# Scaling w1 and w2 apart, through a shared float32 staging, with the first x2 block taken in early

## The chip, the cores and the metric

One core of one Trainium2 chip runs the whole program. The time is that of one execution on the device, in microseconds (us), and the median over several runs is compared. The engines are PE (matrix products), DVE (vector), ACT (activations, scaled copies), POOL (a second elementwise engine) and SP, whose queue issues the DMAs. Every engine takes its instructions in the order in which the program lists them.

## What is computed

Three stages in a row, in float32 to the outside:

```python
q_pool = q.reshape(B, H, S // 2, 2, D).mean(axis=3)       # 4 batches, 8 heads, 1152 keys, D = 64
attn   = softmax(q_pool @ k.T / sqrt(D))
x      = (attn @ v)  as (2304 tokens, 512)
h = x @ w_in;  x = (h * sigmoid(h)) @ w_out               # "MoE1": 512 -> 2048 -> 512
h = (x @ w1) * (x @ w2) @ w3                              # "MoE2": 512 -> 1024, 1024 -> 1024
out = h @ w2_out                                          # 1024 -> 512
```

The weights arrive as float64. The kernel multiplies w3 by w2_out first (eight products of line 1172), so MoE2 has two steps for a block of tokens: the products with w1 and w2, and one with the joint matrix w3 w2_out.

## The kernel before

**Numbers.** Most products are made from pairs of float16 parts, a high and a low one, in three terms (high by high, high by low, low by high). To split an array it is scaled by a power of two that comes from its largest magnitude. That costs a fixed chain, written once as `top_mm` (line 380) with `pow2` (line 372): a maximum along each partition, a small product on PE that spreads the 128 maxima to all partitions (line 385, two matmul instructions), a second maximum on DVE (line 388), and four or five tiny DVE instructions that make the scale. Then ACT writes the high part, and DVE the low one as the scaled difference.

**float64 weights.** A tile of 128 by 512 float64 words is loaded into a buffer `v64` (line 1071), POOL shapes the low words (line 403), ACT the high words (line 409), and DVE merges both in two instructions (lines 413 and 414). For w1 and w2 the result lands in float32 staging tiles `w32`, sixteen of them in the kernel before; ACT then takes their maxima (line 1082). Only when all sixteen are there does `split16` (line 1037) make one scale, `ws2`, for both matrices and split them into `w1h` and `w2h` (lines 1051 and 1058). w2_out becomes `wor` (lines 1092 and 1097), w3 becomes `w3t` (lines 1152 and 1157).

**Blocks.** MoE1 works on nine blocks of 256 tokens (products of lines 816 and 857) and stores its output to memory in HBM, `x2d` (line 872). MoE2 works on six blocks of 384 tokens: `x2s` is loaded (line 1256), its maximum is taken (line 1276) and spread (line 385), the parts `x2h` are written (lines 1290 and 1270), then eight pairs of products follow (line 1311, twelve matmuls each), whose results are evacuated by ACT into `asb` (line 1330) and multiplied by DVE into `abf` (line 1335); the split of that into `abr` feeds the products of line 1389, whose results ACT evacuates (line 1406) and SP stores.

**Room.** SBUF is reused in steps. When the last attention buffer is done, `opened` (line 1012) lets the pools of MoE2's weights be laid over the attention's, and six more PSUM banks (`mt`) become free for products. When MoE1's input weights have been used for the last time, `x2_room` (line 1137) opens the room for `x2s`, `x2h` and `x2m`. When all of MoE1 is done, `done1` opens the room for w3 and the products' results. `blocks` (line 1227) later hands the sixteen `w32` tiles to `abr` and `abf` as eight further buffers each.

**Order.** The order of the instructions is not written by hand. Each step is an operation of a class `Plan` with an engine, an assumed cost, a key and its dependences. `go` (line 176) places operations one by one, always the one that can start first, by key among equals; the order of their planned starts is the order in the program, on all engines at once. `run` repeats this with keys disturbed by the seeded draws listed in `DRAWS` (line 31). So an assumed cost has no effect on the chip but through the order: an operation whose inputs are later on the chip than in the plan makes its engine wait, with all that is queued behind it. The plan's cost for a merge of a float64 tile is 1.65 us (line 418), for the maximum of an x2 block 1.75 us (line 1275).

## Time and profile before

| | us |
|---|---|
| median of 3 runs | 1133.23 (1132.26 to 1133.62) |
| the profiled execution, its own time | 1134.38 |
| its span, first to last instruction | 1132.6 |
| PE busy | 1081.3 |
| DVE busy | 786.5 |
| ACT busy | 695.6 |
| POOL busy | 158.4 |

The profile has one row for each instruction or group of instructions. A row of the timeline gives the start, the duration, the engine, the line, the operation and what it writes from what; in square brackets stands how long the engine sat idle before it, and what ended that. The view of the chain that ended last follows the work back from the last instruction, so that its pieces add up to the span. A view by stretches gives busy times of the engines and the TensorE clock that was granted, as a share of full speed.

### The profile page before, as it was taken

To read this page: it belongs to the slowest core of one execution; us is meant where nothing else is said; L and a number is where in the kernel's file an instruction comes from. 1 tells how busy PE (TensorE), PEld (TensorE's weight loads), DVE (VectorE), ACT (ScalarE), POOL (GpSimd) and SP (SyncE) were. 2 spreads that over 40 slices of the span, in tenths; PEclk is the share of its full clock that TensorE was granted. 3 is DMA by queue.
4 is the path that set the end of the run, shared out by engine and by line. 5 is a ranking of instruction groups with operands and counts; after the bars stand their busy time and mean duration, and the time that the engine had idled before them with its cause. 6 is when DMAs were issued, how large, how long until landed. Compare 5 with 4: busy or idle time off the path is not lost. (4 is left out here: it accounts for less than half of the span.)

```text
span 1132.6 us, 22742 instructions
## 1 busy us (share of the span) xinstructions
PE 1081.3 (95%) x9354; PEld 822.7 (73%) x9354; DVE 786.5 (69%) x1291; ACT 695.6 (61%) x1103; POOL 158.4 (14%) x150
## 2 busy tenths in 40 slices
PE   6767999999999999999999999997999999999998
PEld 5556877788888888887887888886777655556553
DVE  6998996698688898788997784779855542332211
ACT  5767686687687687686877775675644542433322
POOL 1311210021110011120030120555110000000000
PEclk9988999999999999999999999998999999999999
DMA  9746334598989999889999788566331010100001
GB/s 369 268 141 235 129 120 161 124 180 172 199 156 190 224 184 224 183 163 198 216 192 179 138 140 155 202 207 190 128 112 29 29 56 1 56 19 10 28 1 56
DMA packets 294823, 163.21 MB, mean 144 GB/s; under 512 B 256064, under 2 KB 266816, under 8 KB 294720
## 3 DMA queue, kind: packets, MB, share of 16 engines
q1 hardware_dynamic: 294720, 161.77, 59.9%
q8 instruction: 73, 1.20, 0.4%
q14 instruction: 30, 0.25, 0.1%
HBM read 80.22 MB, written 9.44 MB: 79 GB/s over the span
## 5 line engine op out<-in xcount | busy, mean ns | idle before, releaser
L628 DVE TENSOR_REDUCE sm<-sc 128x1 f32<-128x1152 f32 x144 | 192.8, 1351 | 49.2 <-PE sc L582 48.9
L603 ACT ACTIVATE e<-sc,sm 128x1152 f32<-128x1152 f32 x144 | 175.3, 1218 | 77.3 <-DVE sm L628 67.6
L582 PE MATMUL sc<-kt,qt 64*128 64x384 f32 (+3 forms) x1280 | 185.6, 429 | 10.1 <-DMA kt<-in_k_dram 6.4
L857 PEld LDWEIGHTS <-w 128*128 128x128 f16 x1728 | 166.5, 99 | 30.4 <-issue 10.4
L816 PEld LDWEIGHTS <-w 128*128 128x128 f16 x1728 | 167.2, 98 | 28.2 <-issue 8.5
L857 PE MATMUL mm<-g,w 128*128 128x256 f16 x1536 | 181.9, 275 | 0.4 <-ACT x32t L759 0.4
L841 POOL TENSOR_TENSOR g<-t,g 128x512 f16<-128x512 f32 x72 | 97.7, 1363 | 537.0 <-ACT g L838 528.0
L582 PEld LDWEIGHTS sc<-kt,qt 64*128 64x128 f32 (+1 forms) x1280 | 139.2, 178 | 44.3 <-issue 17.6
L614 DVE SCALAR_TENSOR_TENSOR p<-e,sm,p 128x1152 f16<-128x1152 f32 x108 | 153.9, 1440 | 16.8 <-ACT p L649 16.3
L816 PE MATMUL mm<-x,w 128*128 128x256 f16 x1416 | 164.3, 275 | 0.3 <-DVE x L748 0.2
L649 ACT ACTIVATE p<-e,sm 128x1152 f16<-128x1152 f32 x108 | 133.0, 1248 | 17.6 <-DMA pt<-p 13.1
L733 PE MATMUL mm<-pt,v 128*64 128x256 f16 (+1 forms) x1944 | 89.1, 248 | 4.5 <-DMA pt<-p 3.2
L733 PEld LDWEIGHTS <-v 128*64 128x64 f16 x1944 | 80.7, 111 | 13.1 <-issue 9.2
L1311 PEld LDWEIGHTS <-w1h 128*128 128x128 f16 x576 | 56.1, 98 | 37.9 <-issue 0.8
L1311 PEld LDWEIGHTS <-w2h 128*128 128x128 f16 x576 | 56.0, 98 | 37.5 <-issue 1.1
L1311 PE MATMUL mt<-x2h,w2h 128*128 128x384 f16 x456 | 78.4, 326 | 0.0
L1311 PE MATMUL mt<-x2h,w1h 128*128 128x384 f16 x420 | 73.0, 326 | 0.0
L640 PE MATMUL sc<-identr,e 128*128 128x128 f32 x324 | 47.3, 299 | 20.0 <-ACT e L603 17.4
L640 PEld LDWEIGHTS sc<-identr,e 128*128 128x128 f32 x324 | 39.7, 153 | 26.9 <-ACT e L603 21.4
L832 ACT ACTIVATE t<-mm,xm 128x512 f32<-128x512 f32 x59 | 40.4, 685 | 25.3 <-PE mm L816 20.4
L838 ACT ACTIVATE g<-t 128x512 f16<-128x512 f32 x72 | 44.0, 623 | 8.5 <-DVE t L835 8.5
L643 ACT COPY pt<-sc 128x1152 f32<-128x1152 f32 x36 | 39.8, 1114 | 14.3 <-PE sc L640 13.9
(182 smaller groups left out, 1306.1 us busy)
## 6 DMA issues: line engine op xcount, KB each, us to landing
v<-in_moe_w_dram SPq DMA_DIRECT2D x32, 512.0 KB, 4.2
qs<-in_q_dram SPq DMA_DIRECT2D x16, 640.0 KB, 4.9
kt<-in_k_dram SPq DMA_DIRECT2D x16, 576.0 KB, 4.9
qs<-in_q_dram SPq DMA_DIRECT2D x16, 512.0 KB, 4.5
g<-in_moe_w_in_dram SPq DMA_DIRECT2D x16, 512.0 KB, 5.8
w<-t SPq DMA_DIRECT2D x32, 256.0 KB, 3.1
stage<-in_v_dram SPq DMA_DIRECT2D x12, 576.0 KB, 5.0
x2d<-t SPq DMA_DIRECT2D x36, 128.0 KB, 2.3
```

Of the source, the lines that this page charges most:

```text
L582: return nc.tensor.matmul(sc.t[cols, bank, x0 - bank * (S // 3) : x1 - bank * (S // 3)], qt.t[rows * D : (rows + 1) * D, 4 if last else 2 ...
L603: nc.scalar.activation(e.t.rearrange("p (a x) -> p a x", a=3), flat(), AF.Exp, bias=sm.t[:, 0:1], accum_out=sm.t[:, 1:2])
L614: nc.vector.scalar_tensor_tensor(p16.t[:, 1], e.t, sm.t[:, 3:4], p16.t[:, 0], op0=ALU.mult, op1=ALU.subtract)
L628: DVE, 1.36, lambda: nc.vector.tensor_reduce(sm.t[:, 0:1], flat(), axis=AX.XY, op=ALU.max, negate=True),
L640: nc.tensor.transpose(to[:, c * P : (c + 1) * P], e.t[:, c * P : (c + 1) * P], ident)
L649: ACT, 1.27, lambda: nc.scalar.activation(p16.t[:, 0], e.t, AF.Copy, scale=sm.t[:, 3:4]),
L733: nc.tensor.matmul(ps.t[a * D : (a + 1) * D, :nn], v16.t[:, a, c, tv, :], rhs, start=idx == 0, stop=idx == 3 * NK - 1,)
L816: nc.tensor.matmul(ps.t[:, f % 2 * BL : (f % 2 + 1) * BL], w16[0][ct * NQ + f // 4][:, tw, (f % 4) * P : (f % 4 + 1) * P], x16.t[:, ct, tx ...
L838: nc.scalar.activation(gv(0), two(g32), AF.Copy)
L841: nc.gpsimd.tensor_tensor(gv(1), two(g32), gv(0), op=ALU.subtract)
L857: nc.tensor.matmul(ps.t[:, :BL], w16[1][f][:, tw, ct * P : (ct + 1) * P], gs[u].t[:, f % 4, tg, :], start=f == 0 and n == 0, stop=f == NF ...
L1311: nc.tensor.matmul(ps.t[:, :TB], buf.t[:, ct, tw, f * P : (f + 1) * P], xr.t[:, ct, tx, :], start=idx == 0, stop=idx == 11,)
```

## The change

- **Two scales.** The jobs for w1 come first, then those for w2, with half of the w2_out tiles behind each. `split16` runs twice, over eight staging tiles each, with a scale `ws2s[0]` for w1 and `ws2s[1]` for w2. A block's output scale becomes two columns (one more small DVE instruction for each block); the evacuation of w1's products uses one, that of w2's the other.
- **Shared staging.** `w32` has eight tiles in place of sixteen. w2's tiles go where w1's were, so a merge for w2 waits until a tile of w1 has been split.
- **First x2 block early.** `x2s`, one `x2h` buffer and `x2m` move into a pool that is laid when `opened` allows it. The load and the maximum of an x2 block depend on `opened` where they depended on `x2_room`; the second `x2h` buffer still comes with `x2_room`.
- **Further buffers.** `abr` takes its eight further buffers from the eight `w32` tiles, `abf` takes its eight from the `v64` tiles, after the last float64 tile has been read.
- **The schedule.** In the plan, the spreading product of `top_mm` is taken as ready 3.0 us after the maximum that it reads (`SLACK`). The plan's cost of a merge becomes 1.95 us for the jobs of w1, w2, w2_out and w3, and 1.60 us for MoE1's (1.65 us for all before). `DRAWS` is another list, of 33 seeds in place of 23, so the order of the whole program is another.

```diff
@@ -28,9 +28,11 @@
 ENGINES = (PE, ACT, DVE, POOL, SP)
 LOAD_AFTER = 3.0
+SLACK = 3.0
 DRAWS = (
...
 SWITCH = 0.1
 AFTER = {PE: 0.25, ACT: 0.2, DVE: 0.15, POOL: 0.2, SP: 0.0}
@@ -65,7 +67,7 @@
 class Op:
     __slots__ = (
         "eng", "cost", "land", "fn", "key", "after", "need", "ready", "start", "end", "takes", "bufs", "n", "hook",
-        "placed", "mode", "frees",
+        "placed", "mode", "frees", "slack",
     )
@@ -79,7 +81,7 @@
         o = Op()
         o.eng, o.cost, o.land, o.fn, o.key = eng, cost, land, fn, key
         o.after, o.need, o.ready, o.takes, o.bufs, o.placed = [], 0, 0.0, [], [], []
-        o.n, o.hook, o.mode = len(self.ops), None, mode
+        o.n, o.hook, o.mode, o.slack = len(self.ops), None, mode, 0.0
         before = set()
         seen = set()
         for items, write in ((r, False), (w, True)):
@@ -237,7 +239,7 @@
                     buf.tag.free[buf.place] = buf.end
                     buf.tag.last[buf.place] = buf.users
             for x in o.after:
-                x.ready = max(x.ready, o.end + (0.0 if x.eng == e and o.land is None else AFTER.get(e, 0.0)))
+                x.ready = max(x.ready, o.end + x.slack + (0.0 if x.eng == e and o.land is None else AFTER.get(e, 0.0)))
                 x.need -= 1
                 if x.need == 0:
                     cand[x.eng].append(x)
@@ -386,9 +388,10 @@
             [r], [am], key,
         )
         op(DVE, 0.22, lambda: nc.vector.reduce_max(dst(), am.t[:, :P], axis=AX.X), [am], [w], key)
+        spread.slack = SLACK
         return spread
-    def from_f64(dst, words, dst_b, words_b, key):
+    def from_f64(dst, words, dst_b, words_b, key, cost=1.6):
@@ -415,7 +418,7 @@
         op(POOL, 0.8, top3, [], [(words_b, 0)], key - 0.5)
         op(ACT, 0.68, rebias, [(words_b, 1)], [dst_b], key)
-        op(DVE, 1.65, merge, [(words_b, 0), (words_b, 1)], [dst_b], key + 0.01)
+        op(DVE, cost, merge, [(words_b, 0), (words_b, 1)], [dst_b], key + 0.01)
     tiles = []
@@ -988,9 +991,9 @@
     pools = {}
     t_w1, t_w2, t_wor = Tag(1), Tag(1), Tag(1)
-    t_w32 = Tag(4 * NC)
-    ws2 = const.tile([P, 5], F32, name="ws2")
-    ws2_b, wm2_b, wm2 = Buf(Tag(1)), Buf(Tag(1)), wmx[0]
+    t_w32 = Tag(2 * NC)
+    ws2s = [const.tile([P, 5], F32, name=f"ws2_{n}") for n in range(2)]
+    ws2_bs, wm2_b, wm2 = [Buf(Tag(1)) for _ in range(2)], Buf(Tag(1)), wmx[0]
     assert NF == 4 * NC
     t_w64b, t_wfb = Tag(4), Tag(4, fifo=False)
     NR = 3
@@ -1003,12 +1006,17 @@
         pw = pools["pw"] = tc.alloc_tile_pool(name="pw", bufs=1, side="left")
         t_w1.tiles = [pw.tile([P, NC, 2, NF2 * P], F16, name="w1h")]
         t_w2.tiles = [pw.tile([P, NC, 2, NF2 * P], F16, name="w2h")]
-        t_w32.tiles = [pw.tile([P, 512], F32, name=f"w32_{i}") for i in range(4 * NC)]
+        t_w32.tiles = [pw.tile([P, 512], F32, name=f"w32_{i}") for i in range(2 * NC)]
         pf = pools["pf"] = tc.alloc_tile_pool(name="pf", bufs=1, side="left")
         t_wor.tiles = [pf.tile([P, NF2, 2, DM], F32R, name="wor")]
         t_w64b.tiles = [pf.tile([P, 512, 2], I32, name=f"v64_{i}") for i in range(4)]
         t_wfb.tiles = [pf.tile([P, 512], F32, name=f"wfb_{i}") for i in range(4)]
-
+        t_x2s.tiles = [pf.tile([P, NC, TB], F32, name="x2s")]
+        t_x2h.tiles = [pf.tile([P, NC, 2, TB], F16, name="x2h_0")]
+        t_x2m.tiles = [pf.tile([P, 6], F32, name=f"x2m_{i}") for i in range(2)]
+
+    TB = 3 * P
+    t_x2s, t_x2h, t_x2m = Tag(1), Tag(1), Tag(2)
     opened = control(attn_bufs, to_moe2, hook=lambda at: t_mm.free.update({2 + i: at for i in range(6)}))
     attn_end = B * TPB + 2.0
@@ -1019,24 +1027,29 @@
     w1_b, w2_b, wo_b = Buf(t_w1), Buf(t_w2), Buf(t_wor)
     jobs = []
-    for ct in range(NC):
-        for wsrc, buf in ((w1, w1_b), (w2, w2_b)):
+    for n, (wsrc, buf) in enumerate(((w1, w1_b), (w2, w2_b))):
+        for ct in range(NC):
             for u in range(2):
                 cs = slice(512 * u, 512 * (u + 1))
                 jobs.append((wsrc[ct * P : (ct + 1) * P, cs], buf, ct, cs))
-    for j in range(NF2):
-        jobs.append((w2_out[j * P : (j + 1) * P, :], wo_b, j, slice(0, DM)))
+        for j in range(NF2 // 2 * n, NF2 // 2 * (n + 1)):
+            jobs.append((w2_out[j * P : (j + 1) * P, :], wo_b, j, slice(0, DM)))
     for f in range(NF2):
         for u in range(2):
             jobs.append((w3[f, u], None, f, u))
     rows = {}
-    late_bufs = []
+    late_bufs, w64s = [], []
     w32 = []
-    def split16(key):
-
-        op(DVE, 0.2, lambda: nc.vector.reduce_max(ws2[:, 0:1], wm2, axis=AX.X), [wm2_b], [ws2_b], key)
+    def split16(key, n):
+
+        ws2, ws2_b = ws2s[n], ws2_bs[n]
+        cols = slice(2 * NC * n, 2 * NC * (n + 1))
+        op(
+            DVE, 0.2, lambda: nc.vector.reduce_max(ws2[:, 0:1], wm2[:, cols], axis=AX.X),
+            [(wm2_b, c) for c in range(cols.start, cols.stop)], [ws2_b], key,
+        )
         top_mm(lambda: ws2[:, 4:5], lambda: ws2[:, 0:1], ws2_b, ws2_b, key)
         def scales():
@@ -1045,7 +1058,7 @@
             nc.vector.tensor_scalar_mul(ws2[:, 1:2], ws2[:, 1:2], 2.0 ** -28)
         op(DVE, 0.8, scales, [ws2_b], [ws2_b], key)
-        for wf, buf, r_, cs in sorted(w32, key=lambda x: x[3].start):
+        for wf, buf, r_, cs in sorted(w32[cols], key=lambda x: x[3].start):
             op(
                 ACT, 0.64,
                 lambda wf=wf, buf=buf, r_=r_, cs=cs: nc.scalar.activation(
@@ -1066,12 +1079,13 @@
         src, buf, r_, cs = jobs[c]
         w64, wf = Buf(t_w64b), Buf(t_w32 if buf in (w1_b, w2_b) else t_wfb)
         late_bufs.extend((w64, wf))
+        w64s.append(w64)
         late_op(
             opened, SP, 0.5,
             lambda: nc.sync.dma_start(w64.t.rearrange("p n t -> p (n t)"), src.bitcast(I32)),
             [], [(w64, 0), (w64, 1)], key - 2, land=4.5,
         )
-        from_f64(lambda: wf.t, lambda: w64.t, wf, w64, key)
+        from_f64(lambda: wf.t, lambda: w64.t, wf, w64, key, 1.95)
         if buf in (w1_b, w2_b):
             junk = Buf(t_wfb)
             late_bufs.append(junk)
@@ -1082,8 +1096,8 @@
                 lambda: nc.scalar.activation(junk.t, wf.t, AF.Abs, accum_out=wm2[:, n_ : n_ + 1]),
                 [wf, wmx_b[0]], [junk, (wm2_b, n_)], key + 0.1,
             )
-            if len(w32) == 4 * NC:
-                split16(key + 0.2)
+            if len(w32) % (2 * NC) == 0:
+                split16(key + 0.2, len(w32) // (2 * NC) - 1)
             return
         if buf is None:
             rows[(r_, cs)] = wf
@@ -1105,8 +1119,7 @@
     for c in range(len(jobs) - 2 * NF2 + NR):
         job(c, key)
         key += 0.46
-    TB = 3 * P
-    t_w3r, t_w3t, t_x2s, t_x2h, t_x2m = Tag(1), Tag(1), Tag(1), Tag(2), Tag(2)
+    t_w3r, t_w3t = Tag(1), Tag(1)
     t_asb, t_abf, t_abr, t_abm = Tag(2), Tag(8), Tag(8), Tag(2)
     w3f_b, w3m_b, w3m = Buf(Tag(1)), Buf(Tag(1)), wmx[1]
     assert NF >= NF2 + 4
@@ -1130,11 +1143,9 @@
     def to_x2():
         winp.release()
         px = pools["px"] = tc.alloc_tile_pool(name="px", bufs=1, side="left")
-        t_x2s.tiles = [px.tile([P, NC, TB], F32, name="x2s")]
-        t_x2h.tiles = [px.tile([P, NC, 2, TB], F16, name=f"x2h_{i}") for i in range(2)]
-        t_x2m.tiles = [px.tile([P, 5], F32, name=f"x2m_{i}") for i in range(2)]
-
-    x2_room = control(w16_b[0], to_x2)
+        t_x2h.tiles.append(px.tile([P, NC, 2, TB], F16, name="x2h_1"))
+
+    x2_room = control(w16_b[0], to_x2, hook=lambda at: t_x2h.free.update({1: at}))
     plan.link(x2_room, {opened})
     c_next = len(jobs) - 2 * NF2 + NR
@@ -1216,15 +1227,18 @@
         key3 += 0.2
     def to_blocks():
-        w32_ = t_w32.tiles
-        t_abr.tiles.extend(w32_[j][:, :TB].bitcast(F16).rearrange("p (t x) -> p t x", t=2) for j in range(NF2))
-        t_abf.tiles.extend(w32_[NF2 + j][:, :TB] for j in range(NF2))
-
-    def more(at):
-        for tag in (t_abr, t_abf):
-            tag.free.update({8 + j: at for j in range(NF2)})
-
-    blocks = control([wf for wf, _, _, _ in w32], to_blocks, hook=more)
+        for tile_ in t_w32.tiles:
+            t_abr.tiles.append(tile_[:, :TB].bitcast(F16).rearrange("p (t x) -> p t x", t=2))
+
+    def to_blocks_f():
+        for tile_ in t_w64b.tiles:
+            whole = tile_.rearrange("p n t -> p (n t)").bitcast(F32)
+            t_abf.tiles.extend(whole[:, u * 512 : u * 512 + TB] for u in range(2))
+
+    blocks = control(
+        [wf for wf, _, _, _ in w32[2 * NC :]], to_blocks, hook=lambda at: t_abr.free.update({8 + j: at for j in range(8)})
+    )
+    blocks_f = control(w64s, to_blocks_f, hook=lambda at: t_abf.free.update({8 + j: at for j in range(8)}))
     last_bufs, bounds, ends = [], [], []
     def out_rows(w):
@@ -1257,7 +1271,7 @@
         early = key - 10.0 if bk else attn_end + 6.0
         late_op(
-            x2_room, SP, 0.5 * len(segs), load,
+            opened, SP, 0.5 * len(segs), load,
             [(x2_b[seg], ct) for seg, _, _, _ in segs for ct in range(NC)], [xs], early, land=5.5,
         )
@@ -1272,19 +1286,20 @@
             )
         late_op(
-            x2_room, DVE, 1.75,
+            opened, DVE, 1.75,
             lambda xs=xs, xm=xm: nc.vector.reduce_max(xm.t[:, 0:1], xs.t, axis=AX.XY, apply_absolute_value=True),
             [xs], [(xm, 0)], early + 1,
         )
         top_mm(lambda xm=xm: xm.t[:, 1:2], lambda xm=xm: xm.t[:, 0:1], (xm, 0), (xm, 1), early + 1)
         op(DVE, 0.65, scales, [(xm, 1)], [(xm, 2)], early + 1)
-        op(
-            DVE, 0.15,
-            lambda xm=xm: nc.vector.tensor_scalar(
-                xm.t[:, 4:5], xm.t[:, 2:3], ws2[:, 1:2], None, op0=ALU.mult
-            ),
-            [(xm, 2), ws2_b], [(xm, 3)], early + 1.5,
-        )
+        for n in range(2):
+            op(
+                DVE, 0.15,
+                lambda xm=xm, n=n: nc.vector.tensor_scalar(
+                    xm.t[:, 4 + n : 5 + n], xm.t[:, 2:3], ws2s[n][:, 1:2], None, op0=ALU.mult
+                ),
+                [(xm, 2), ws2_bs[n]], [(xm, 3 + n)], early + 1.5,
+            )
         op(
             ACT, 1.55,
             lambda xs=xs, xr=xr, xm=xm: nc.scalar.activation(xr.t[:, :, 0], xs.t, AF.Copy, scale=xm.t[:, 3:4]),
@@ -1333,10 +1348,10 @@
             def both(pb_=pb_, asb=asb, abf=abf, xm=xm):
                 nc.vector.scalar_tensor_tensor(
-                    abf.t, pb_.t[:, :TB], xm.t[:, 4:5], asb.t, op0=ALU.mult, op1=ALU.mult
+                    abf.t, pb_.t[:, :TB], xm.t[:, 5:6], asb.t, op0=ALU.mult, op1=ALU.mult
                 )
-            late_op(done1, DVE, 0.57, both, [pb_, asb, (xm, 3)], [abf], key)
+            late_op(done1, DVE, 0.57, both, [pb_, asb, (xm, 4)], [abf], key)
             late_op(
                 done1, ACT, 0.5,
                 lambda abf=abf, abr=abr, am=am, f=f: nc.scalar.activation(
```

## Rows read from the trace of the kernel before

**Rows 1.** The page: the span.

```profile
span 1132.6 us, 22742 instructions
```

**Rows 2.** Stretches: length; busy PE, PEld, DVE, ACT, POOL (instructions); granted clock; DMA share; GB/s.

```profile
0.00:113.30 113.30, 81.25 (x543) 62.95 (x544) 97.25 (x161) 74.08 (x108) 22.17 (x34) 0.88 0.71 253
113.30:780.40 667.10, 658.35 (x6915) 555.01 (x6913) 544.92 (x854) 476.17 (x694) 121.55 (x100) 1.00 0.82 176
780.40:786.40 6.00, 0.01 (x1) 0.04 (x1) 5.97 (x7) 1.93 (x3) 3.93 (x4) 0.91 0.74 240
786.40:792.00 5.60, 5.60 (x26) 4.10 (x27) 5.36 (x16) 3.40 (x4) 0.79 (x2) 0.50 0.41 123
792.00:1128.00 336.00, 336.00 (x1874) 200.63 (x1872) 133.02 (x257) 139.30 (x295) 9.98 (x12) 1.00 0.13 44
```

**Rows 3.** Waits of PE over the span: us in total, times, longest.

```profile
PE sc L640 <- ACT e L603: 17.4, 9, 3.4
...
PE mt L385 <- DVE x2m L1276: 6.0, 1, 6.0
PE mm L385 <- DVE sm L608: 5.2, 1, 5.2
```

**Rows 4.** The chain that ended last: start, us, what, matmuls.

```profile
786.39 0.77 PE mt L385 x2
787.16 7.71 PE mm L857 x48
794.87 2.62 PE mt L857 x24
...
847.92 0.22 PE mm L385 x2
```

**Rows 5.** Timeline of DVE around and after the wait: start, us, line, operation.

```profile
734.71 1.53 DVE L414 SCALAR_TENSOR_TENSOR w<-v,w 128x512 int32<-128x512 int32 x1
...
756.35 1.53 DVE L414 SCALAR_TENSOR_TENSOR w<-v,w 128x512 int32<-128x512 int32 x1
758.73 0.17 DVE L1039 TENSOR_REDUCE ws<-wmx 128x1 f32<-128x16 f32 x1 [0.85 <-ACT wfb L1082]
...
784.31 0.28 DVE L388 TENSOR_REDUCE ws<-mt 128x1 f32<-128x128 f32 x1
784.51 1.74 DVE L1276 TENSOR_REDUCE x2m<-x2s 128x1 f32<-128x1536 f32 x1
...
792.60 2.46 DVE L1058 SCALAR_TENSOR_TENSOR w1h<-w,ws,w1h 128x512 f16<-128x512 f32 x3
...
798.71 1.41 DVE L1058 SCALAR_TENSOR_TENSOR w2h<-w,ws,w2h 128x512 f16<-128x512 f32 x2 [0.46 <-ACT w2h L1051]
...
860.87 0.69 DVE L414 SCALAR_TENSOR_TENSOR wfb<-v,wfb 128x512 int32<-128x512 int32 x1
...
876.92 0.62 DVE L1335 SCALAR_TENSOR_TENSOR w<-mt,x2m,asb 128x384 f32<-128x384 f32 x1 [0.34 <-PE mt L1311]
```

**Rows 6.** SP's queue: the first x2 block's load, its start and issue time.

```profile
769.67 1.27 SPq L1256 DMA_DIRECT2D x2s<-x2d  x2
```

**Rows 7.** The tile x2s, 760 to 800 us: time from issue to landing.

```profile
DMA to landing us min/median/max: 4.4/5.4/5.9
```

**Rows 8.** DVE groups, 709 to 800 us: count, busy us, mean ns, idle before.

```profile
L414 DVE SCALAR_TENSOR_TENSOR w<-v,w 128x512 int32<-128x512 int32 x16 | 16.4, 1027 | 0.5
L413 DVE SCALAR_TENSOR_TENSOR w<-w,v 128x512 int32<-128x512 int32 x16 | 14.8, 924 | 8.2 <-POOL v L403 5.3 <-ACT w L409 1.6 <-issue 1.3
```

**Rows 9.** Line 413, 709 to 860 us: durations ns, least, median, greatest.

```profile
L413 DVE SCALAR_TENSOR_TENSOR w<-w,v x16: 679/693/1644, 713.9 to 754.7; 128x512 int32<-128x512 int32 x16
```

**Rows 10.** ACT's timeline: the maximum of the eighth w1/w2 tile in order.

```profile
736.27 0.63 ACT L1082 ACTIVATE wfb<-w 128x512 f32<-128x512 f32 x1 [2.41 <-DVE w L414]
```

**Rows 11.** PE's timeline: MoE1's first product, and the first with w2.

```profile
105.74 4.59 PE L816 MATMUL mm<-x,w 128*128 128x256 f16 x24
...
801.90 2.11 PE L1311 MATMUL mt<-x2h,w2h 128*128 128x384 f16 x12
```

**Rows 12.** The chain that ended last, at the last block.

```profile
1102.20 12.95 PE mt L1389 x60
```

2 lines of the change are left out of this document (removed), and 3 rows, old and new, of the table DRAWS.

## The prediction

> **What bounds the kernel now.** I read the stretches first. From 792.0 to 1128.0 us PE is busy for 336.00 of 336.00 us, from 113.3 to 780.4 us for 658.35 of 667.10; only the first 113.3 us leave much open, 32.05 us [rows 2]. So PE sets the end, and a change can gain only where PE stands still, runs at the low clock, or has work taken away. The one hole in the region that this change touches is 780.4 to 786.4 us: PE is busy 0.01 of 6.00 us there, DVE 5.97 [rows 2]. The waits name it: line 385, the spread of an x2 block's maximum, waited 6.0 us for line 1276 [rows 3].
>
> The hole costs more than its length. Right behind it the granted clock is 0.50, the lower of the two levels (1.2 GHz), where it is 1.00 in the stretch from 792.0 us on [rows 2]. The chain shows the price: 48 matmuls of line 857 took 7.71 us, while 24 soon after took 2.62, so 48 at full clock are 5.24; the spread itself took 0.77 where one at full clock takes 0.22 [rows 4]. That is 2.47 + 0.55 = 3.02 us, and with the wait 9.02 us.
>
> Why was the maximum late? Its load was issued at 769.67 us [rows 6], after MoE1's input weights had been used for the last time, and landed within 4.4 to 5.9 us of an issue [rows 7], so by about 777. DVE reached the maximum at 784.51 [rows 5]: it was DVE's queue, not the data. The plan puts a merge at 1.65 us; the sixteen for w1 and w2 took 1.027 + 0.924 = 1.95 us each [rows 8]. Sixteen times 0.30 us put DVE 4.8 us behind the plan, and the merges for w2_out add to that. The spread stood in PE's queue where the plan had it, ahead of MoE1 products that were ready.
>
> **The change part by part.**
>
> **First x2 block early.** Its load needs `opened` and the MoE1 blocks 0 and 1, stored long before. Removed is the wait for `x2_room`; moved with it are two DMAs on SP (1.27 us of issue [rows 6]), the maximum (1.74 us of DVE [rows 5]), the spread, the scale and the two parts. In SP's queue the two DMAs now stand among the loads of line 1071, which they can hold back by their issue and by the time of their own transfer, at most about the 4.4 to 5.9 us of a landing [rows 7]; the spare worked out below hides that, and without it up to 5.9 us of lateness would reach w2's parts. In exchange the weight loads that stood behind 769.67 us no longer wait for MoE1. On DVE the maximum can be done anywhere from about the first merge of w1 or w2 at 713.9 us [rows 9] to 780, a stretch in which DVE was not full: the first-merge group alone had 8.2 us of idle before it [rows 8].
>
> **Slack and merge cost.** These move places in the queues and add no instruction. The spread is planned 3.0 us after its maximum, and a merge at 1.95 us, which is what the rows show. Both act against the error that made the hole. The cost is that a spread comes later than it could, and the scale behind it: nothing where PE has other products ready (after 113.3 us), up to 3.0 us each where it has not. Ahead of MoE1's first product, at 105.74 us [rows 11], the program has two such spreads (scale of w_in, scale of MoE1's first block): bound of a loss 2 x 3.0 = 6.0 us. On the other side stands a wait of 5.2 us at just such a spread [rows 3] (line 385, MoE1's weights), which a later place could fill with other work: bound of a gain 5.2 us. Most of the early idle is neither (17.4 us are transposes that wait for the exponentials [rows 3]), and DVE is busy 97.25 of the first 113.3 us [rows 2], so work shifted there mostly changes places. I take zero, and keep both ends.
>
> **The redrawn order** touches everything. From 113.3 to 780.4 us PE idles 8.75 us [rows 2]; another order can lose or save a few of these. I take zero here too, since nothing in the trace says which.
>
> **A scale each.** One more maximum (0.17 us [rows 5]), spread (0.22 us of PE [rows 4]), second maximum (0.28 us [rows 5]), scale, and one tiny instruction per block on DVE. On the path lies only PE's 0.22 us.
>
> **Shared staging** is the new wait. w2's first merge waits for a split of w1, that for w1's scale. Queued behind the waiting merge on DVE is whatever the plan put there; who waits in the end is PE, at the first product with w2. From rows: the eighth merge ended at 734.71 + 1.53 = 736.24 us [rows 5]; its maximum on ACT at about 737.1 [rows 10]; maxima, spread and scale about 1.4 us, with slack 3.0 more: 741.5; a first tile split by about 743. The other eight merges took from 736.24 to 756.35 + 1.53 = 757.88, 21.6 us [rows 5], so to 764.6; maximum, scale and slack to about 769.8; four splits of the first half, at half of the 7.5 us from 792.60 to 798.71 + 1.41 [rows 5], to 773.6. Needed is it at 801.90 [rows 11] less 9.0, so 792.9: 19.3 us to spare. The other bound: the x2 work, the w2_out tiles and MoE1's own steps push it back to where it was, 800.12 us [rows 5], and PE waits 7.2 us. The rows of the second eight merges already hold such neighbours, and much of DVE's load of 780 to 800 us is what now moves ahead, so I take no wait and keep 7.2 for the range.
>
> **Further buffers.** The extra `abf` now come free after the last merge, which ended at 861.6 us; the first of them was written at 876.92 [rows 5]. 15 us of cover: nothing. **At the end** the last block's spread may move 3.0 us back; behind it stood 12.95 us of PE's products without a gap [rows 12], more than the scale and the first parts need: nothing.
>
> **Sum.** -9.02 + 0.22 = -8.8 us. The profiled execution took 1134.38 us, 1.78 more than its span [rows 1], and lies 1.15 us above the median of the runs; its own time would become 1125.6, and the median 1133.2 - 8.8 = 1124.4 us.
>
> **The rivals.**
>
> *The early part gains too.* The 5.2 us wait at the weights' spread [rows 3] fills, or part of it and of the mid waits: 1124.4 - 5.2 = 1119.2. For: slack aims at every spread. Against: DVE is the fuller engine there.
>
> *The change doesn't do what it says.* The maximum or w2's scale still comes late against PE's order, as keys and draws decide where it stands, and PE stops at the spread or at w2's parts for up to 7.2 us: 1124.4 + 7.2 = 1131.6, a little less for a shorter wait. For: DVE had no room from 780.4 to 786.4 us [rows 2]. Against: the x2 step may now stand anywhere in some 66 us.
>
> *The early order loses.* Two spreads later by 3.0 each, MoE1's first product later by 6.0: 1130.4, and beyond where the redrawn order adds mid waits.
>
> *Slower: w2's chain.* The place is PE's first product with w2, the price what the chain is late there. The sixteen merges were between 0.68 and 1.64 us in their first instruction [rows 9], and a full one reached 1.64 + 1.53 = 3.17 us against 1.95 [rows 5, 8, 9], while POOL worked. Moved to where block 8's POOL steps lie, eight merges could cost 8 x 1.22 = 9.8 us more. On top of the late bound that is a wait of 7.2 + 9.8 = 17.0 us: 1141.4. It decides from w2's first half later than 792.9 + 8.8 = 801.7 us; half of the added price gives 1136.5. Against: from the early bound the same 9.8 us end at 783.4, inside the spare.
>
> The Trainium skill (SBUF — State Buffer, section "SBUF: two separate sides") speaks for this rival: it has a vector instruction with two SBUF inputs and a GpSimd one that reads SBUF take a shared port pair in turns, the loser standing for the whole instruction. By that rule it is the overlap with POOL, not a length of the merge, that decides, and 1136.5 is what half of the merges caught would give. The greatest durations agree with it, 1.64 against a median of 0.69 us [rows 9].
>
> **How the numbers follow.** Chances: forecast 0.50, early gain 0.12, wait come back 0.14, early loss 0.14, w2's chain 0.10. What a measurement of this kernel can tell from no change is about 0.2%, 2.3 us, so faster means below 1130.9. The first two lie there whole, and of the third and fourth 0.07 and 0.05: 0.74. Within 0.2%: 0.05, 0.03 and, of the chain, 0.03: 0.11. Slower: 0.02, 0.06 and 0.07: 0.15. The forecast's own range is 1121 to 1128, for the redrawn order's few us. To leave no more than 2 in 10 out, the range goes down to 1118 (the early gain) and up to 1135 (the wait come back, most of the early loss, and the mild end of the chain).
>
> **What would show it.** Right: no wait of line 385 for line 1276 over 1 us, PE busy without a gap from about 710 us to the last product, granted clock 1.00 throughout there, the x2 maximum before 780 us, w1's splits before w2's merges end, and about 32 us of PE idle in the first 113 us. Wrong: a new gap at line 1311's first product with w2 or at a spread of `ws2`; merges for w2 over 2.5 us on average; or MoE1's first product later than 108 us, with a gap of PE before it. If the gap is gone and the time hardly moves, the gain went into the first 113 us or the middle, and the stretches would say which.

## The result, and the profile after

The changed kernel takes 1117.89 us in the median (1115.92 to 1120.33), the kernel before beside it 1133.42 (1132.26 to 1133.89): a ratio of 0.9866, with a 95% interval of 0.9844 to 0.9887. That is 15.5 us less. The forecast was 8.8 us less, so the sign was right, and 6.7 us, three quarters of the forecast, were not in the sum. The time lies on the lower edge of the range 1118 to 1135 (1118.0, if the ratio is put on the 1133.2 that the forecast started from), and below the forecast's own 1121 to 1128. The profiled execution of the changed kernel took 1118.18 us, its span is 1116.4, against 1134.38 and 1132.6 [rows 1]: 16.2 us between the spans, which the stages below divide up.

The stages are set off by PE's own milestones: the end of the last attention product, the start of the first MoE2 product, the end of the span.

| | before | after | difference |
|---|---|---|---|
| last attention product ends at | 706.2 | 695.5 | -10.7 |
| from there to MoE2's first product | 93.7 | 88.9 | -4.8 |
| from there to the end | 332.7 | 332.0 | -0.7 |

The view by stretches of the kernel after (length; busy PE, PEld, DVE, ACT, POOL; granted clock; DMA share; GB/s):

```profile
0.00:113.30 113.30, 82.67 (x612) 63.16 (x614) 99.69 (x172) 76.80 (x112) 20.78 (x32) 0.95 0.70 242
113.30:695.50 582.20, 574.80 (x6173) 483.90 (x6173) 487.87 (x775) 421.53 (x591) 82.38 (x62) 1.00 0.87 178
695.50:784.40 88.90, 86.25 (x774) 76.54 (x775) 75.22 (x101) 60.35 (x117) 45.71 (x42) 0.98 0.56 181
784.40:1116.40 332.00, 327.46 (x1802) 193.31 (x1800) 129.17 (x259) 133.76 (x286) 11.45 (x14) 1.00 0.14 47
723.30:729.00 5.70, 5.69 (x38) 4.41 (x38) 4.60 (x8) 3.89 (x9) 3.60 (x4) 0.71 0.72 220
```

The same view of the kernel before, cut at its own milestones:

```profile
113.30:706.20 592.90, 584.39 (x6241) 489.10 (x6240) 485.93 (x786) 426.25 (x594) 78.21 (x60) 1.00 0.85 173
706.20:799.90 93.70, 87.47 (x775) 77.09 (x773) 76.72 (x98) 60.67 (x117) 49.92 (x46) 0.96 0.59 192
799.90:1132.60 332.70, 328.20 (x1802) 193.59 (x1800) 126.61 (x249) 134.56 (x286) 8.12 (x10) 1.00 0.13 42
```

First stage: in the first 113.3 us PE now does 612 matmuls, where it did 543 [rows 2]. So less is left for the stretch behind: 574.80 us of PE's work in place of 584.39 (9.6 less), with 7.4 us of idle in place of 8.5 (1.1 less). That is the 10.7. In the first 113.3 us itself PE's idle fell only from 32.05 [rows 2] to 30.63. PE did more there with nearly the same busy time, at a granted clock of 0.95 in place of 0.88 [rows 2].

Second stage: the hole is gone, but a new one has come. The waits of PE over the span (us in total, times, longest), then PE's timeline and DVE's around the stages:

```profile
PE sc L643 <- ACT e L606: 11.3, 8, 4.0
PE sc L585 <- ACT pt L646: 11.0, 10, 2.4
PE sc L585 <- DVE qt L468: 6.7, 1, 6.7
...
PE mt L860 <- POOL g L844: 2.4, 1, 2.4
```

```profile
695.71 5.40 PE L819 MATMUL mm<-x,w 128*128 128x256 f16 x48 [0.23 <-DVE x L751]
...
723.31 2.50 PE L860 MATMUL mt<-g,w 128*128 128x256 f16 x11 [2.43 <-POOL g L844]
...
755.15 0.39 PE L387 MATMUL mt<-identr,x2m 128*128 128x128 f32 x2
...
784.20 0.39 PE L387 MATMUL mm<-identr,ws 128*128 128x128 f32 x2
784.42 2.11 PE L1326 MATMUL mt<-x2h,w1h 128*128 128x384 f16 x12
...
792.09 5.81 PE L1183 MATMUL mt<-wor,w3t 128*128 128x512 f32 x24
797.74 4.07 PE L1326 MATMUL mt<-x2h,w2h 128*128 128x384 f16 x24
```

```profile
718.81 1.74 DVE L1290 TENSOR_REDUCE x2m<-x2s 128x1 f32<-128x1536 f32 x1
...
738.70 2.06 DVE L1071 SCALAR_TENSOR_TENSOR w1h<-w,ws,w1h 128x512 f16<-128x512 f32 x3
...
790.83 0.74 DVE L1071 SCALAR_TENSOR_TENSOR w2h<-w,ws,w2h 128x512 f16<-128x512 f32 x1
794.36 2.08 DVE L1071 SCALAR_TENSOR_TENSOR w2h<-w,ws,w2h 128x512 f16<-128x512 f32 x3
```

The x2 maximum runs at 718.81 where it ran at 784.51 [rows 5], its spread at 755.15 without a wait, and w1's parts are made 54 us earlier (738.70 against 792.60 [rows 5]). The new wait is PE's, 2.43 us for the low part of MoE1's activations, which POOL writes (tile `g`, line 844), with a granted clock of 0.71 in the 5.7 us behind it. w2's chain is late: its scale is spread behind MoE1's last product (784.20), the first half is ready at 796.44, PE's first product with it starts at 797.74. PE has no gap there, because the order puts four products with w1 and one of w3 by w2_out (5.81 us) ahead.

### The profile page after: what moved, and what is told of

It reads as the page before. It is cut to its first block, busy times and chain, and to the rows that moved or that the text cites. A ratio compares the mean times of both kernels' runs of the same rounds, so it can differ in the third digit from the quotient of the medians.

```text
span 1116.4 us, 22719 instructions
## 1 busy us (share of the span) xinstructions
PE 1071.2 (96%) x9356; PEld 816.9 (73%) x9356; DVE 792.0 (71%) x1304; ACT 692.4 (62%) x1103; POOL 160.3 (14%) x150
## 4 chain that ended last, share of the span: by engine, by line
PE 53%; DMA 4%; DVE 1%; POOL 1%; issue 0%; ACT 0%; ACTq 0%; POOLq 0%; SPq 0%
PE mt L1326 13%; PE mt L1404 6%; PE mm L819 6%; PE mm L860 6%; PE sc L585 4%; PE mm L1326 4%; PE mm L736 4%; DMA pt<-p 3%; PE mt L1183 3%; PE mt L860 3%; PE mm L1404 2%; PE mt L819 1%; PE mm L1183 1%; DMA v<-in_moe_w_dram 1%; POOL g L844 1%
## 5 line engine op out<-in xcount | busy, mean ns | idle before, releaser
L585 PE MATMUL sc<-kt,qt 64*128 64x384 f32 (+3 forms) x1280 | 183.1, 427 | 17.8 <-ACT pt L646 11.0
L844 POOL TENSOR_TENSOR g<-t,g 128x512 f16<-128x512 f32 x72 | 100.4, 1402 | 527.9 <-ACT g L841 475.7
L617 DVE SCALAR_TENSOR_TENSOR p<-e,sm,p 128x1152 f16<-128x1152 f32 x108 | 161.2, 1500 | 12.8 <-ACT p L652 12.4
L860 PE MATMUL mm<-g,w 128*128 128x256 f16 x1440 | 167.1, 273 | 0.0
L1326 PE MATMUL mt<-x2h,w1h 128*128 128x384 f16 x444 | 77.1, 326 | 0.0
L643 PE MATMUL sc<-identr,e 128*128 128x128 f32 x324 | 44.6, 286 | 14.4 <-ACT e L606 11.3
L1345 ACT ACTIVATE asb<-mt,x2m 128x384 f32<-128x384 f32 x37 | 20.8, 577 | 54.4 <-PE mt L1326 48.0
L643 PEld LDWEIGHTS sc<-identr,e 128*128 128x128 f32 x324 | 36.7, 146 | 22.7 <-ACT e L606 14.6
```

The lines of the kernel that those rows point to most:

```text
L585: return nc.tensor.matmul(sc.t[cols, bank, x0 - bank * (S // 3) : x1 - bank * (S // 3)], qt.t[rows * D : (rows + 1) * D, 4 if last else 2 ...
L617: nc.vector.scalar_tensor_tensor(p16.t[:, 1], e.t, sm.t[:, 3:4], p16.t[:, 0], op0=ALU.mult, op1=ALU.subtract)
L643: nc.tensor.transpose(to[:, c * P : (c + 1) * P], e.t[:, c * P : (c + 1) * P], ident)
L844: nc.gpsimd.tensor_tensor(gv(1), two(g32), gv(0), op=ALU.subtract)
L860: nc.tensor.matmul(ps.t[:, :BL], w16[1][f][:, tw, ct * P : (ct + 1) * P], gs[u].t[:, f % 4, tg, :], start=f == 0 and n == 0, stop=f == NF ...
L1326: nc.tensor.matmul(ps.t[:, :TB], buf.t[:, ct, tw, f * P : (f + 1) * P], xr.t[:, ct, tx, :], start=idx == 0, stop=idx == 11,)
```

## The experiments

Where an experiment says "order taken over", the keys with which the planner of a kernel ends are written out as a list and the draws are left out, so that this part of the program stands as it does in that kernel:

```diff
-        order = self.timed(keys)
-        for n in DRAWS:
-            keys = self.draw(n, keys, order)
-            order = self.timed(keys)
-        return order
+        return self.timed(list(KEYS))
```

### E1: the spread later, nothing else

Is it enough to move the x2 spread out of PE's way? In the kernel before, after planning:

```diff
-        for o in plan.run():
+        order = plan.run()
+        some = [x2_spreads[0]]
+        for o in put_later(order, some, 6.5):
```

`put_later` sorts the order again with these operations 6.5 us of plan later, and with what depends on them behind them, on every engine.

> The kernel before, with one step put later in the order: the spread of the first x2 block's maximum, with what depends on it, 6.5 us of plan later, behind five MoE1 products that are ready. If the hole's price is simply lost time (6.0 us of waiting and 3.0 us at the low clock), the time is 1133.4 - 9.0 = 1124.4 us. The rival: DVE was full during the hole and is late next, so PE arrives earlier at the first products with w1 and w2 (at about 791 us) and waits there for their parts, which DVE does not finish before about 797: a new wait of some 6 us at line 1311, and 1130 us or more.

Measured: 1134.72 us, ratio 1.0009 [0.9993, 1.0026]: no gain. The waits of PE in E1, the stretch around them, and DVE's second maximum for x2, in E1 and then in before with the last of the first four splits of w1:

```profile
PE mt L1322 <- ACT x2h L1301: 2.9, 1, 2.9
...
PE mt L1322 <- DVE x2h L1281: 1.9, 1, 1.9
PE mt L1322 <- DVE w1h L1069: 0.6, 1, 0.6
```

```profile
780.00:806.00 26.00, 20.68 (x153) 15.02 (x151) 23.38 (x39) 15.80 (x27) 6.37 (x7) 0.87 0.48 152
```

```profile
792.48 0.29 DVE L399 TENSOR_REDUCE x2m<-mt 128x1 f32<-128x128 f32 x1
```

```profile
788.09 0.28 DVE L388 TENSOR_REDUCE x2m<-mt 128x1 f32<-128x128 f32 x1
...
796.09 0.83 DVE L1058 SCALAR_TENSOR_TENSOR w1h<-w,ws,w1h 128x512 f16<-128x512 f32 x1 [1.03 <-ACT w1h L1051]
```

The wait of 6.0 us became 2.9 + 1.9 + 0.6 = 5.4 us at MoE2's first products, still behind the x2 parts and w1's, and the clock is 0.87 there. So the row that names the wait [rows 3] named the first victim of a late chain. The chain (maximum, scale, parts of x2 and of w1) has to come earlier; this later place gains nothing. The test isn't of PE's order alone, though: the spread came 1.4 us later than in before (787.82 against 786.39 us), but DVE took the second maximum 4.4 us later, because the edit puts the x2 scale and parts back in DVE's queue too. So a share of the new waits is the edit's own. The w1 parts set a floor: PE had no MoE1 products left from 792.1 us on, and even in before's order the fourth part of w1 is done only at 796.92, so about 4 us of waiting would have stood in any case.

### E2 and E3: the two halves of the change crossed

E2 has the kernel before's data path (one scale, sixteen staging tiles, x2 late), and takes over after's order for attention and MoE1. E3 has the changed data path and the changed plan for MoE2, and takes over before's order for attention and MoE1. In E2 the slack and the cost of 1.60 us hold ahead of MoE2 only. In E3 the slack holds from MoE2 on only, and MoE1's merges are planned at the old 1.65 us:

```diff
-        spread.slack = SLACK
+        spread.slack = SLACK if len(plan.ops) >= 2156 else 0.0
```

> The data path of the kernel before (one scale, sixteen staging tiles, x2 room late), with the attention and MoE1 in the order of the kernel after (its final keys, slack and merge cost for these stages alone; MoE2's steps keep the old keys, moved by a constant). If the order of the attention is where two thirds of the gain are, the attention ends at about 695.5 us where it ended at 706.2, and the time is 1133.4 - 10.7 = 1122.7 us, with a hole before MoE2's products still open. If the gain came from the data path, it stays at 1133.

> The data path of the kernel after, with its slack and merge cost for MoE2, but with the attention and MoE1 in the order of the kernel before (its final keys, no slack and the old merge cost there). If the order of the attention is worth 10.7 us and the rest 5.5 us, the attention ends at 706.2 us and the time is 1133.4 - 5.5 = 1127.9 us. If the data path makes the attention faster, 1118.

E2: 1124.47 us, 0.9918 [0.9895, 0.9940]. E3: 1125.94 us, 0.9936 [0.9913, 0.9958]. PE's timeline of E2, then of E3, and E3's stretches:

```profile
695.42 5.40 PE L1058 MATMUL mm<-x,w 128*128 128x256 f16 x48 [0.23 <-DVE x L990]
...
775.50 0.52 PE L626 MATMUL mm<-identr,x2m 128*128 128x128 f32 x2 [4.30 <-DVE x2m L1518]
```

```profile
707.39 5.40 PE L1059 MATMUL mm<-x,w 128*128 128x256 f16 x48 [0.23 <-DVE x L991]
...
792.10 4.06 PE L1566 MATMUL mt<-x2h,w1h 128*128 128x384 f16 x24
...
805.41 4.08 PE L1566 MATMUL mt<-x2h,w2h 128*128 128x384 f16 x24
```

```profile
738.00:770.00 32.00, 31.96 (x294) 28.48 (x292) 31.59 (x44) 25.18 (x50) 18.27 (x17) 1.00 0.53 174
770.00:792.10 22.10, 22.10 (x204) 19.78 (x203) 21.72 (x32) 13.02 (x24) 12.77 (x11) 1.00 0.62 200
707.20:792.10 84.90, 84.67 (x774) 75.64 (x774) 76.96 (x102) 59.40 (x116) 48.13 (x42) 1.00 0.60 198
```

E2 starts MoE1's last blocks at 695.42, as after does (695.71), and still has a wait at the x2 spread (4.30 us, line 626 there). E3 starts them at 707.39, as before does, and needs 84.9 us from the last attention product (707.2) to MoE2's first, with no gap but the 0.23 us at its start and the clock at 1.00: 8.8 us less than the 93.7 of before. So the gain has two parts: about 9 us come from the order of attention and MoE1, which the old data path takes as well, and 7 to 8 us from what the change is about. By the ratios they sum to 0.0082 + 0.0064 = 0.0146, 16.5 us of 1133.4; within the intervals that is the 15.5 us of after. The wait for POOL comes with the order: E2, with the old data path, has it too (1.9 us for `g`), and E3 doesn't.

E3's stretches also show what is next. DVE is busy 31.59 of 32.00 and 21.72 of 22.10 us: the room that the change opened is used up.

### E5, E6, E7: what of the data path it is

All three are E3 with something of the change taken back. E5: x2 waits for `x2_room` again, no slack, merges planned at 1.65 us, so that only the two scales and the shared staging are left. E6: x2 early, but no slack and 1.65 us. E7: slack and 1.95 us, but x2 late. The two edits (E5 has both, E6 the first, E7 the second):

```diff
-        spread.slack = SLACK if len(plan.ops) >= 2156 else 0.0
+        spread.slack = 0.0
...
-        from_f64(lambda: wf.t, lambda: w64.t, wf, w64, key, 1.95)
+        from_f64(lambda: wf.t, lambda: w64.t, wf, w64, key, 1.65)
```

```diff
-            opened, SP, 0.5 * len(segs), load,
+            x2_room, SP, 0.5 * len(segs), load,
...
-            opened, DVE, 1.75,
+            x2_room, DVE, 1.75,
```

> The kernel of the run before with the old attention order and the new data path, of which three parts are undone: the load and the maximum of an x2 block wait for x2_room again, no slack at MoE2's spreads, merges at 1.65 us in the plan. What is left of the change is a scale each and the shared staging. All keys as they were. If the early x2 block is what takes the hole away, its load again starts at about 770 us, the maximum comes after PE is ready for it, and a wait of 3 to 6 us at the spread (or at the parts of x2) is back: 1131 to 1134 us. If it is enough that w1 is split early, so that DVE is ahead, PE waits under 1 us and the time stays at 1126 to 1128.

> The same kernel with the x2 block early, but without slack at MoE2's spreads and with merges at 1.65 us in the plan, all keys as they were. If slack and cost only guard an order that already has room, no new wait over 1 us and 1126 us, as with them. If they took the hole away, a wait of some us at a spread comes back: 1129 or more.

> The same kernel with slack and the dearer merges, but the load and the maximum of an x2 block wait for x2_room. All keys as they were; the plan now has PE's first MoE2 product 1.7 us later. If room early is needed, the load starts at about 770 us and PE waits 1.5 to 6 us, at the x2 block's parts or its spread: 1128 to 1133 us. If the slack is enough, 1126 to 1127.

| | us | ratio to before |
|---|---|---|
| E5, two scales alone | 1130.96 | 0.9983 [0.9973, 0.9994] |
| E6, two scales and x2 early | 1129.23 | 0.9970 [0.9952, 0.9989] |
| E7, two scales, slack and costs | 1127.91 | 0.9953 [0.9935, 0.9970] |
| E3, all of these | 1125.94 | 0.9936 [0.9913, 0.9958] |

PE's timeline of E5, of E6 and of E7, where it waits behind the attention:

```profile
737.75 0.49 PE L627 MATMUL mt<-identr,ws 128*128 128x128 f32 x2 [2.88 <-DVE ws L1290]
...
782.76 0.46 PE L627 MATMUL mm<-identr,x2m 128*128 128x128 f32 x2 [1.30 <-DVE x2m L1530]
```

```profile
737.62 0.49 PE L627 MATMUL mt<-identr,ws 128*128 128x128 f32 x2 [2.40 <-DVE ws L1290]
```

```profile
792.33 1.95 PE L1566 MATMUL mt<-x2h,w1h 128*128 128x384 f16 x11 [1.77 <-DVE x2h L1524]
```

The two scales alone shorten the x2 wait to 1.30 us and bring a new one, 2.88 us at w1's scale, planned behind merges that are longer on the chip than in the plan. Slack and the true cost remove that wait (it is there in E5 and E6, in E7 and E3 it isn't). x2 early removes the wait at the x2 spread (in E5, not in E6) or at the x2 parts (in E7, not in E3). Between E5 and E3 lie 5.0 us with intervals apart. The single steps are smaller than their intervals, which overlap, so how the 5.0 us divide between slack and early x2 is told by the waits alone, not by the times.

### E8: has w2's chain room to spare?

E3, with the second merge instruction of w2's eight tiles done three times (`again` is 2 for them and 0 for all others):

```diff
-            nc.vector.scalar_tensor_tensor(di, hi, SIGN, di, op0=ALU.bitwise_and, op1=ALU.bitwise_or)
+            for _ in range(1 + again):
+                nc.vector.scalar_tensor_tensor(di, hi, SIGN, di, op0=ALU.bitwise_and, op1=ALU.bitwise_or)
```

> The same kernel with early x2, slack and the dearer merges, and with the second merge instruction of each of w2's eight tiles done three times (it changes nothing the second time): 16 x 0.69 = 11 us more on DVE between w1's split and w2's scale, in an unchanged order. By the prediction's working the chain of w2 has 19.3 us to spare, and the time stays at 1126 us. By the trace with the old attention order w2's first half was ready at 797.9 us and needed at 805.4, 7.4 us to spare, with DVE busy 53.3 of 54.1 us before: then PE waits 11 - 7.4 = 3.6 us or more, with the low clock behind it, 1129.5 to 1133.

Measured: 1140.26 us, 1.0068 [1.0041, 1.0094], 14.3 us over E3 (the spans, 1137.3 and 1124.1, lie 13.2 apart). The DVE group of that instruction, 709 to 860 us (count, busy us, mean ns, idle before), in E3 and in E8, and E8's waits:

```profile
L657 DVE SCALAR_TENSOR_TENSOR w<-v,w 128x512 int32<-128x512 int32 x16 | 15.9, 995 | 0.5
```

```profile
L658 DVE SCALAR_TENSOR_TENSOR w<-v,w 128x512 int32<-128x512 int32 x32 | 30.9, 967 | 1.1
```

```profile
PE mt L1424 <- ACT w3t L1404: 3.5, 1, 3.5
...
PE mt L1101 <- POOL g L1085: 2.2, 1, 2.2
PE mt L1101 <- ACT g L1082: 2.1, 1, 2.1
PE mt L1424 <- DVE w3t L1409: 1.4, 1, 1.4
```

15.0 us more on DVE cost 13 to 14 us, more than either forecast had. Hardly any of it was hidden. The waits don't stand at w2's products but at MoE1's activations `g` (lines 1082, 1085) and at w3 (lines 1404, 1409). w2's first half is even ready 8 us ahead of its product there (810.22 and 818.60 us). DVE was full (34.21 of 35.00 us from 770 to 805), and everything behind the merges came late.

### E12, E9 and E10: is the low clock of the early part worth anything?

After has a granted clock of 0.95 in the first 113.3 us, before 0.88. If the clock were the cause of the early gain, filling PE's holes there should bring part of it. E12 is the kernel before (order taken over), with 20 products into the spread's own PSUM buffer ahead of the one spread that waits 5.2 us [rows 3]; nothing reads them:

```diff
+        def spread_():
+            for _ in range(fill):
+                nc.tensor.matmul(am.t[:, :P], ident, ident, start=True, stop=True)
+            nc.tensor.matmul(am.t[:, :P], src().to_broadcast([P, P]), ident, start=True, stop=True)
...
-        top_mm(lambda: s_[:, 4:5], lambda: s_[:, 0:1], wst_b[wi], wst_b[wi], key2)
+        top_mm(lambda: s_[:, 4:5], lambda: s_[:, 0:1], wst_b[wi], wst_b[wi], key2, (20, 0)[wi])
```

> The kernel before in an unchanged order, with 20 idle matmuls of two instructions each (4.4 us at full clock) ahead of one spread alone, that of w_in's maximum, for which PE waits 5.2 us. They write the PSUM buffer of the spread itself, which is free, so they lie inside the wait. The wait for DVE stays as long; what can change is the clock behind it, 0.63 from 76.9 to 84.0 us. If the low clock behind a wait is paid in full, the steps there (spread 0.79, 1.16 and 5.84 us, against 0.22, 0.66 and 4.11 at full clock) take 2.8 us less, and the attention ends that much earlier: 1133.4 - 2.8 = 1130.6 us. If PE only reaches the next wait for DVE or ACT earlier, the clock rises and the time stays within 1 us of 1133.4.

Measured: 1133.94 us, 1.0003 [0.9992, 1.0015]. The stretch of the hole and the one behind it, in before and in E12:

```profile
71.70:76.90 5.20, 0.00 (x0) 0.00 (x0) 5.10 (x10) 0.00 (x0) 0.21 (x1) 0.85 0.53 191
76.90:84.00 7.10, 7.09 (x45) 5.08 (x46) 6.69 (x18) 4.98 (x9) 1.09 (x2) 0.63 0.51 154
```

```profile
71.70:76.90 5.20, 5.20 (x46) 4.92 (x44) 4.73 (x9) 1.14 (x3) 0.00 (x0) 1.00 0.33 114
76.90:84.00 7.10, 7.10 (x64) 5.21 (x62) 6.86 (x19) 4.38 (x8) 1.35 (x2) 1.00 0.63 175
```

The clock behind the hole rose from 0.63 to 1.00 and PE did 64 matmuls there in place of 45; MoE1's first product still came at 106.03 us, against 105.74 [rows 11], and the time is the same. PE only reached its next wait sooner. At this place a low clock isn't paid.

E9 (before) and E10 (after) put the same filling ahead of several groups of transposes. The numbers are the group and its count of products:

```diff
+FILL = {1: 20, 3: 12, 6: 14, 7: 12, 11: 14, 13: 19, 17: 24}
...
+                for _ in range(FILL.get(turned[0], 0)):
+                    nc.tensor.matmul(to[:, :P], ident, ident, start=True, stop=True)
```

E9 also fills the hole of E12; E10 has 28, 14, 13 and 8 products at four groups. They gave 1161.54 us, 1.0246 [1.0214, 1.0277], and 1127.48 us, 0.9951 [0.9934, 0.9969], each slower than the kernel they are made from, and tell nothing of the clock's price:

> The kernel before in an unchanged order, with idle matmuls put where PE waits longest in the first 113 us: 20, 12, 14, 12, 14, 19 and 24 of them ahead of seven groups of transposes that wait for the exponentials, 38 ahead of the spread of w_in's maximum. They write what the next product overwrites, and take at most four fifths of each wait at 0.11 us apiece. If the low clock behind those waits is what PE loses most by in this stretch, the granted clock there rises from 0.88 to 0.97 or more and the attention ends 4 to 8 us earlier: 1126 to 1130 us. If PE has to wait for DVE and ACT there anyway, the clock rises, the waits grow by as much, and the time stays at 1133 to 1134. If the fillings themselves hold PE up, it is longer.

> The kernel after in an unchanged order, with 28, 14, 13 and 8 idle matmuls ahead of its four longest early waits for the exponentials (4.0, 2.0, 1.9 and 1.3 us). Its low clock lies in the first 45 us (0.83 in the first 30). If that costs PE time, the clock rises to 0.9 or more there and the time is 1114 to 1117 us; if not, 1118.

PE's timeline of E9:

```profile
13.36 7.19 PE L888 MATMUL sc<-identr 128*128 128x128 f32 x40 [2.72 <-ACT e L850]
```

The fillings write the PSUM buffer that the transposes need, so they wait for the same exponentials and then stand ahead of the transposes: work added, no hole filled.

### E4 and E11: the new wait, and a better order

E4 is after with two of POOL's steps on float64 words (line 406), which stand around the step for `g` that PE waits for, put 4 us of plan later:

```diff
+        some = [o for o in order if o.fn.__name__ == "top3" and 722.0 < o.start < 725.0]
+        for o in put_later(order, some, 4.0):
```

> The kernel after, with two POOL steps that shape float64 words (line 406) put 4 us of plan later, behind the low part of g for which PE waited 2.4 us at 720.9 us. If that wait and the low clock behind it are POOL's order, the wait shrinks to some tenths, the low clock goes, and the time is 1117.9 - 4 = 1114 us. The rival: the shaped words are late for w1's merges and so for w1's scale, or the next step on POOL holds PE as long: 1117 to 1119.

Measured: 1118.26 us, 0.9866 [0.9844, 0.9887], as after. E4's waits:

```profile
PE mt L871 <- POOL g L855: 1.9, 2, 1.0
PE mt L871 <- ACT g L852: 1.6, 2, 1.2
```

The wait of 2.4 us came apart into four short ones, 3.5 us in all, two of them for ACT. The low clock is gone (1.00 from 718 to 735 us), and the time is no shorter. PE seems to be ahead of the whole chain for `g`, not held by one POOL step. So E11 keeps after's data path and mends the plan: POOL's steps at the costs that after shows from one start to the next (1.55 us for `g`, 721.79 to 723.34, where the plan had 1.3, and 1.05 for the words of MoE2's weights, 720.74 to 721.79, where it had 0.8; both from block 7 on), a slack of 1.0 us ahead of MoE1's second products there, and keys searched anew with these costs.

```diff
-        op(POOL, 0.8, top3, [], [(words_b, 0)], key - 0.5)
+        op(POOL, 0.8 if cost < 1.9 else 1.05, top3, [], [(words_b, 0)], key - 0.5)
...
-            op(POOL, 1.3, g_lo, [g32, (gb, (u % 2, 0))], [(gb, (u % 2, 1))], key - 12)
+            op(POOL, 1.3 if blk < 7 else 1.55, g_lo, [g32, (gb, (u % 2, 0))], [(gb, (u % 2, 1))], key - 12)
...
+                if blk >= 7:
+                    o.slack = 1.0
```

> The kernel after with the order searched on: POOL's low part of g at 1.55 us and its shaping of words at 1.05 us in the plan for the last two MoE1 blocks and MoE2, 1.0 us of slack at their products of line 860, and the keys drawn on from those of after; the planned end is 1.2 us earlier, all of it in the attention. If the wait of 2.4 us for POOL and the low clock behind it go, 1117.9 - 4.0 - 1.1 = 1112.8 us. If other waits take its place, 1116 to 1119.

Measured: 1112.66 us, 0.9821 [0.9797, 0.9846]; its interval just touches that of after at 0.9844 to 0.9846, and its runs (1112.1 to 1115.32) all lie below those of after. PE's timeline of E11, and the one wait left behind the attention:

```profile
688.43 3.99 PE L976 MATMUL mm<-pt,v 128*64 128x256 f16 x108
...
777.16 4.06 PE L1568 MATMUL mt<-x2h,w1h 128*128 128x384 f16 x24
```

```profile
PE mt L1425 <- ACT w3t L1405: 0.6, 1, 0.6
```

The attention ends at 692.4, 3.1 us sooner than in after, and 84.7 us later MoE2 begins, as in E3 (84.9) and 4.2 us sooner than in after: that is what the wait for POOL, the clock behind it, and the order around it had cost. The last stage is 1.1 us longer (333.1 us), so E11's gain over after is that of a new order as a whole, not of the one wait.

## Why the prediction was right, and where it wasn't

**The time itself: partly luck.** What came lies nearest to the rival that the early part gains too (1119.2 us, given a chance of 0.12). But that rival had 5.2 us at one wait, and the early part gained 10.7 us, while the stage with the hole gave 4.0 us less than the sum. Two errors against each other put the time as near as it is.

**The hole at the x2 spread: right, and near in size.** The sum's one term, 9.02 - 0.22 = 8.8 us, is what E3 shows in the stage (93.7 to 84.9) and 7.5 us of it in the time. That the two agree to a tenth is chance: the same wait in the same order took 6.0 us in before and 4.6 in E12. In after itself the gain is partly given back: the stage is only 4.8 us shorter, because of the wait for POOL. No step of the working looked at MoE1's chain for `g`, which the redrawn order moves too; "nothing in the trace says which" holds for the place, but a bound of a few us was due, and it stood only in the forecast's own range.

**Why the hole closes: half right.** "It was DVE's queue, not the data" holds. But the working treated the spread as a place in PE's queue, and in E1 a later place there gained nothing. What closes the hole is that w1's parts leave the crowded stretch (two scales), that x2's do, and that the plan knows the merges' true length (E5 to E7).

**The early part: the step that failed.** It was taken at zero, bounded by +6.0 and by -5.2 from one wait, on the ground that DVE is busy for 97.25 of 113.3 us and "work shifted there mostly changes places". Measured is -10.7 us to the end of the attention, and E2 shows it without the new data path. The two views by stretches, from before and from after, tell it:

```profile
60.00:90.00 30.00, 20.71 (x139) 15.33 (x138) 29.09 (x60) 17.81 (x26) 3.94 (x6) 0.86 0.47 152
```

```profile
60.00:90.00 30.00, 25.18 (x202) 18.38 (x201) 29.32 (x53) 18.57 (x28) 3.54 (x5) 1.00 0.37 120
```

DVE is as full in both, with 60 and with 53 instructions, and PE does 139 matmuls in one and 202 in the other. A full DVE fixes how much DVE work fits, not which. An order that puts steps with much PE work for their DVE time early, and leaves the others for the middle, where PE sets the pace and DVE stood still for 107 of 592.9 us in the kernel before, gains what PE does ahead of time. That reading is argued from these two rows, not tested by itself, and the sums up to the end of the attention don't show it as idle time saved. Counted in one stretch, both kernels do the same 6782 matmuls up to there, with PE busy for 81.25 + 584.39 = 665.64 us before and 82.67 + 574.80 = 657.47 us after. So 8.2 of the 10.7 us are the same products in less busy time, with a granted clock of 0.95 in place of 0.88 in the first 113.3 us, and only 2.5 us are less idle. E2 does these matmuls in 658.79 us, E3 in 666.07. The bound should have come from PE's idle of the early stretch, 32.05 us [rows 2], and from its busy time at the low clock there, not from the one wait that a slack could fill. That wait is gone from after's list, but others took its place (11.0 us for `pt`, 6.7 for `qt`), and PE's idle there is only 1.4 us less.

What the cause is, the order's choice of work or the higher clock, stays open: in after the clock is 1.00 from 60 to 90 us and 0.86 in before. The sums put most of the gain into busy time, but E12 warns against taking that for the cause: there the clock rose at one place, and the time came back as waiting. That is no answer for the whole stretch. Nor is it settled whether the draws or the slack there made the order.

**Shared staging: right in result, wrong in its working.** No wait came, but there were no 19.3 us to spare: w2's first half is ready 1.3 us before its product (796.44, 797.74). In E3, whose attention ends 1 us later than before's, it is ready at 797.9 us, 24 us later than the 773.6 of the working, and E8 passes 15.0 us of DVE work on almost whole. The step that failed added up the merges' own spacing from before and left the neighbours out: x2's parts, w1's splits and four w2_out tiles now lie between them (line 1071 at 738.70 stands in that stretch). What hid the lateness was the order (w1's products first, one of w3 by w2_out behind them), and that was not in the working. In E3 the same half (four splits from 795.22 on) is needed only at 805.41. The rival for w2's chain named the right cost and the wrong place: DVE's time is the price, but it is paid by whatever stands behind DVE.

That rival's other leg, merges lengthened further beside POOL, did not come: in after the fourteen merges into w1's and w2's staging between 709 and 800 us took 0.929 + 1.085 us on average, 2.01, against 1.95 [rows 8]. Long ones still stand beside POOL's work: the pair at 722.16 us, with POOL busy but for short gaps from 720.74 to 724.31, took 1.64 + 1.01 us, the pair at 745.83, with POOL idle from 744.71 to 748.81, 0.68 + 0.69. The rule of the Trainium skill on the shared port (SBUF — State Buffer, "SBUF: two separate sides") is thus not contradicted, and it decided nothing here.

**Slack and costs at no price: right, and too small a claim.** They were costed at nothing. E5 and E6 show that without them the two scales make a wait of their own, 2.4 to 2.9 us at w1's scale.

**Further buffers and the end: right.** The last stage is 0.7 us shorter, and no wait for `abr`, `abf` or a last spread is among PE's waits.

**The signs named in advance.** The wait of line 385 is gone, w1's splits come before w2's merges end, and the x2 maximum is at 718.81. "Busy without a gap from about 710 us, the clock at 1.00" is wrong by the 2.43 us at 723 us. "About 32 us of PE idle in the first 113" holds (30.63) and was the wrong thing to watch: the stretch's count of matmuls, 612 against 543, shows the lead that PE had there.

## What to carry to other kernels

A wait names who stopped, not what is late: before its length goes into a sum, see how full the engine behind it is right after, since moving the victim may only find the next one (E1). Where a change redraws the order of the whole program, no stage is "taken at zero": bound each by the idle of its limiting engine and by the price of its low clock, and compare the number of instructions done by a given time and the busy time of the same instructions, not the idle alone. When a change fills a second engine to the brim, test it with work added there (E8): it tells at once whether any slack is left.
